# Attention slots 6 to 12 with one visit each: values in 64x32 tiles beside the next slot's scores

## The chip, the cores and the metric

The kernel runs on one core of one Trainium2 chip. The metric is the device time of one execution in microseconds; lower is better. A core has a matrix engine (TensorE, PE in the profile; its weight loads are PEld), a vector engine (VectorE, DVE), a scalar engine (ScalarE, ACT), a general engine (GpSimd, POOL) and a queue for DMAs (SyncE, SP). The matrix engine works out of on-chip memory (SBUF) into eight accumulator banks (PSUM).

## What is computed

```python
q, k, v: (8, 12, 448, 64)            # batch, heads, sequence, head width
q_n, k_n = rmsnorm(q, g_q), rmsnorm(k, g_k)
scores = 1 / sqrt(64) * q_n @ k_n.T
attn = exp(scores - max) / (sum(exp) + 1e-09)
x = (attn @ v) as (3584, 768)         # token, head * width
h = x @ w_in                          # (768, 2048)
out = (h - tanh(h)) @ w_out           # (2048, 768), float32
```

The weights come as float64; the kernel makes float32 of their two words.

## The kernel before

**Slots.** The attention is cut into 48 slots, one for each batch and pair of heads, six to a batch (`NP` = 6). A slot's probabilities stand with keys on the partitions: three full chunks of 128 keys (c = 0, 1, 2) and 64 last keys (c = `KF` = 3), whose 448 queries are folded into two halves of 224. Scores (`scores`, matmuls L567) are made by tiles of 64x32: 64 rows are one head's width, 32 columns a quarter of the keys, so eight tiles work at once. The exponential (L573, ScalarE) takes them from PSUM to the tiles `p`, `p_full` and `p_last`. The values (`last_values`, L621; `values`, L671; `half_values`, L633) multiply them by v. The sums of the exponentials are either made on TensorE by a matmul with ones (`totals`, L694) and inverted on VectorE (L699), or, from slot 13 on, on VectorE and ScalarE (`fold` and what follows it). `divide` multiplies the values by the inverted sums and writes x.

**Two ways for the values.** `values` uses tiles of 128x32 (all 128 keys of a chunk at once) with 224 columns moving, one bank for each half of the queries. `visit`, which slots from `FOLDED` = 13 on use, has tiles of 64x32 as the scores have: each half of a chunk's keys goes to a bank of its own (`half_values`), 448 columns moving, and the matmuls stand in waves between those of the next slot's scores. The two banks then hold two partial sums, so `divide` copies the first to SBUF on ScalarE (L755), adds the second on VectorE (L756) and then multiplies (L760).

**The order of the work** is written out by hand: `first_slot` for slots up to 5, `early_slot` for 6 to 11, `slot` from 12 on. Between its steps each calls `run(ns)`, which issues so much of the MLP, a generator of matmuls priced at its TensorE time. A slot has about four gaps of MLP (`gap_ns`). In slots 6 to 8 the MLP is the first product of batch 0 (`hidden`, matmuls L839, in seven block products p in the order 1, 5, 6, 2, 3, 7, 4 on three banks, whose results VectorE takes at L908 to L922 and ScalarE at L886 and L906); in slots 9 to 11 it is `project_first` (L1256), 96 matmuls of 448 columns, 16 to a bank, copied by ScalarE (L1262) and turned by VectorE (L948). From slot 12 it is batch 1.

**What else runs there.** Weight pieces are loaded (L287, L291, on SP, into three raw buffers), rounded by ScalarE (L71, L72), then VectorE (L78, L79, L82), then GpSimd (L90), after which the raw buffer may be loaded anew. VectorE makes sums of weight blocks (L354, L378 to L381). For the slots to come, q and k are loaded (L101 to L125) four slots ahead and v two, squared by ScalarE (L130, L131), reduced by VectorE (`norm`, L140, L141), brought to the power -1/2 by GpSimd (L142), scaled (`norm_q`, L452 on ScalarE for slots 9 to 14) and turned (`turn`, L465 and L469). From slot 10 on the sums of the full chunks are made on VectorE first (`add`, L598 and L604; `add_last`, L611), and `totals` has only those to multiply. In the last three slots of batch 1, `divide` also sets off four sums of x on GpSimd (L791).

**Banks.** Five banks (`sc`) turn round for scores, totals, turns and values, three (`mm`) for the MLP. Before slot 12 the last two of the five become `av_banks`, for values alone, and three remain to turn round.

The steps of `early_slot(s)` before the change: `totals(s)`, scores of s+1 for chunks 0 and 1, load of v, a gap, turn of s+2, squares of s+3, loads of q and k, a gap, scores of s+1 for the last keys, values of s, `divide(s)`, scores of chunk 2, then half a gap ahead of each of `add`, `add_last`, `norm` and `norm_q`.

Of the kernel before, what the change touches and what calls it, by code (L numbers as in the profile page):

```python
# [13 lines left out]
ALU = mybir.AluOpType  # L14
# [130 lines left out]
def bounded_path(tc, ctx, q, k, v, moe_w_in, moe_w_out, out, g_col, ident, ones, half_ones, neg_half, early):  # L145
# [74 lines left out]
    def load(s, names):  # L220
        b, hp = steps[s]
        for name in names:
            src = {"q": q, "k": k, "v": v}[name]
            if s == 0 and name != "v":
                t = early[name]
            else:
                if name == "v":
                    t = nat.tile([P, 2, NCH, D], F32, name="v_nat", bufs=3)
                elif name == "q":
                    rows = loaded["rows", s] = qk_rows()  # L230
                    t = rows[:CP, : 2 * NCH * D].rearrange("p (h c d) -> p h c d", h=2, c=NCH)
                else:
                    rows = loaded.pop(("rows", s))
                    t = rows[:, 2 * NCH * D :].rearrange("p (c h d) -> p c h d", c=NCH, h=2)
                fetch(nc, name, t, src[b, 2 * hp : 2 * hp + 2], in_order(s))
            loaded[name, s] = t
# [200 lines left out]
    def squares(s):  # L437
        squares_of(nc, early["sq"], early["n"], loaded["q", s], loaded["k", s])
# [42 lines left out]
    def by_blocks(s):  # L481
        return has(s) and s >= TURNED
# [67 lines left out]
    def sc_bank():  # L550
        return bank_of("sc")
# [61 lines left out]
    def last_values(s, av):  # L613

        v_nat, p = loaded["v", s], probs[s, KF]
        for n in range(2):
            keys, at = slice(n * KR, (n + 1) * KR), n * HS if s >= FOLDED else 0
            for m in range(2):
                for h in range(2):
                    r = (2 * m + h) * BL  # L620
                    nc.tensor.matmul(  # L621
                        av[n][r : r + BL, at : at + HS], lhsT=v_nat[keys, h, KF, m * BL : (m + 1) * BL],
                        rhs=p[keys, h, 0], start=(s < FOLDED), stop=False, skip_group_check=(s >= FOLDED),
                    )

    def half_values(s, c, av, first):
# [52 lines left out]
    def totals(s, dn):  # L679

        parts = [t[:, h, n * HS : (n + 1) * HS] for t in sums.get(s, ()) for n in range(2) for h in range(2)]
        parts = [(parts, [ones[:, :BL]] * 2)] if parts else []
        if not sums.pop(s):
            for p in full(s):
                parts.append(
                    ([p[:, h, n * HS : (n + 1) * HS] for n in range(2) for h in range(2)], [ones[:, :BL]] * 2)
                )
            last = probs[s, KF]
            parts.append(([last[:, h, 0] for _ in range(2) for h in range(2)], [half_ones[:, n] for n in range(2)]))
        for i, (moving, by) in enumerate(parts):  # L690
            for n in range(2):
                for h in range(2):
                    r = (2 * n + h) * BL
                    nc.tensor.matmul(  # L694
                        dn[r : r + BL, :HS], lhsT=by[n], rhs=moving[2 * n + h],
                        start=(i == 0), stop=(i == len(parts) - 1),
                    )
        rs = whole[s] = sp.tile([P, HS], F32, name="rs")
        nc.vector.reciprocal(rs, dn[:, :HS])  # L699


    FOLDED = 2 * NP + 1

    def fold(s):

# [41 lines left out]
    def divide(s, av):  # L747
        b, hp = steps[s]
        rs = whole.pop(s)
        if b > PAIRED and b % 2 and hp == 1:  # L750
            x = xT[b, hp] = late["blocks"].tile([P, S], F32, name="xT_more", bufs=1)
        else:
            x = xT[b, hp] = xp.tile([P, S], F32, name="xT")
        if s >= FOLDED:
            nc.scalar.copy(out=x, in_=av[0][:, :S])  # L755
            nc.vector.tensor_tensor(out=x, in0=x, in1=av[1][:, :S], op=ALU.add)  # L756
        for m in range(2):
            rows = slice(m * D, (m + 1) * D)
            if s >= FOLDED:
                nc.vector.tensor_tensor(out=x[rows], in0=x[rows], in1=rs, op=ALU.mult)  # L760
                continue
            for n in range(2):
                nc.vector.tensor_tensor(
                    out=x[rows, n * HS : (n + 1) * HS], in0=av[n][rows, :HS], in1=rs[n * D : (n + 1) * D],
                    op=ALU.mult,
                )
        for c in range(NCH):
            del probs[s, c]
        if b < PAIRED and hp >= HC:
            c = hp - HC  # L770
            x_sums(b, (c,), range(4), nc.vector if b == 0 and c == HC - 1 else nc.gpsimd)
# [526 lines left out]
    def run(ns):  # L1298

        spent[1] += ns  # L1300
        while spent[0] + 1.0 < spent[1]:
            took = next(stream, None)
            if took is None:
                return
            spent[0] += took
# [15 lines left out]
    def has(s):  # L1321
        return 0 <= s < NS
# [40 lines left out]

    def early_slot(s):
        gap = gap_ns(s)
        totals(s, sc_bank())
        if has(s + 1):
            scores(s + 1, 0)
            scores(s + 1, 1)
        if has(s + 2):  # L1370
            load(s + 2, "v")
        run(gap)
        if has(s + 2):
            turn(s + 2, sc_bank(), sc_bank())
        if has(s + 3):
            squares(s + 3)
        if has(s + 4) and not by_blocks(s + 4):
            load(s + 4, "qk")
        run(gap)
        if has(s + 1):  # L1380
            scores(s + 1, KF)
        av = [sc_bank() for _ in range(2)]
        last_values(s, av)
        divide(s, values(s, av))
        if has(s + 1):
            scores(s + 1, 2)
        for work, n in ((add, 1), (add_last, 1), (norm, 3), (norm_q, 3)):
            run(gap / 2)
            if has(s + n):
                work(s + n)  # L1390

    def slot(s):

        gap = gap_ns(s)
        av = av_banks
        if has(s + 1):
            scores(s + 1, KF)
        if s < FOLDED:
            last_values(s, av)
            totals(s, sc_bank())  # L1400
            divide(s, values(s, av))
            for c in range(KF):
                scores(s + 1, c)
        else:
            visit(s, av)
        if has(s + 2):
            load(s + 2, "v")
        rows, ahead, following = has(s + 2), has(s + 3), has(s + 1)
        folded = following and s + 1 >= FOLDED
        first = s + 3 == TURNED  # L1410
        scaled = rows and not first
        if scaled:
            power_blocks(s + 2)
        work = (
            (
                (following, lambda: add(s + 1, False)), (first, lambda: turn(s + 2, sc_bank(), sc_bank())),
                (ahead and not first, lambda: load_blocks(s + 3)),
            ),
            (
                (following, lambda: add_third(s + 1)), (first, lambda: load_blocks(s + 3)),  # L1420
                (True, lambda: x_sums_later(s, 0)),
            ),
            ((following, lambda: add_last(s + 1)),),
            ((folded, lambda: fold(s + 1)),),
            ((folded, lambda: fold_rest(s + 1)), (True, lambda: x_sums_later(s, 1))),
            ((scaled, lambda: scale_blocks(s + 2)),),
            ((folded, lambda: gather(s + 1, 0)), (ahead, lambda: square_blocks(s + 3))),
            ((scaled, lambda: turn_blocks(s + 2, 0)), (folded, lambda: gather(s + 1, 1))),
            ((scaled, lambda: turn_blocks(s + 2, 1)), (ahead, lambda: norm_blocks(s + 3))),
            ((folded, lambda: spread_sums(s + 1)), (True, lambda: x_sums_later(s, 2))),  # L1430
            ((scaled, lambda: weigh_keys(s + 2)), (ahead, lambda: meet_blocks(s + 3))),
            ((folded, lambda: widen_sums(s + 1)),),
            ((folded, lambda: turn_sums(s + 1)),),
            (),
        )
        for point in work:
            run(4 * gap / (len(work) + 1))
            for wanted, fn in point:
                if wanted:
                    fn()  # L1440
        run(4 * gap / (len(work) + 1))
# [4 lines left out]
    done[0] = 1  # L1446
    for s in range(-3, NP):
        first_slot(s)
    for s in range(NP, 2 * NP):
        early_slot(s)  # L1450
    banks["sc"], av_banks = banks["sc"][:3], banks["sc"][3:]
    for s in range(2 * NP, NS):
        slot(s)
    run(1e9)
# [345 lines left out]
```

## Time and profile before

| | us |
|---|---|
| median of three runs | 1360.98 (1359.57 to 1361.94) |
| the profiled execution | 1361.07 |
| its span in the profile | 1359.3 |
| TensorE busy | 1318.1 (97%) |
| VectorE busy | 956.4 (70%) |
| ScalarE busy | 557.4 (41%) |
| GpSimd busy | 762.9 (56%) |
| start of slots 8, 9, 10, 11 and 12 on TensorE | 145.1, 176.0, 208.8, 240.6, 272.3 |

The page has the busy time of each engine, the span in 40 slices of 34 us with the busy share in tenths, the chain of work that ended last, and groups of instructions by line. A matmul of float32 appears as two. "TensorE <- VectorE L910" reads: idle until that instruction ended. Lines of the timeline give start, length, engine, source line, operation, what is written and read, and in brackets the idle time ahead of it with its releaser. TensorE's clock was at its full rate through slots 6 to 12.

### The profile page before, as it was taken

The page shows a single profiled execution, that of the slowest core. Times are in us where ns is not written, and L with a number is a line of the kernel's source. Part 1 is how long each engine was busy: PE and PEld are TensorE (multiplying, and loading weights), DVE is VectorE, ACT ScalarE, POOL GpSimd, SP SyncE. Part 2 cuts the span into 40 slices and gives each one's busy share as a digit, 9 for nine tenths or more (in the row PEclk, how much of TensorE's full clock was granted, in tenths as well). Part 3 has the DMA queues.
Part 4 walks back from the last instruction along what each step waited for, and adds up shares of the span by engine and source line. Part 5 has one row for each costly group of instructions (what it writes and reads, how often), then busy time and mean ns, then how long its engine had stood idle before and what let it go on. Part 6 is the DMA issues. An engine that isn't in the chain of part 4 may idle for free.

```text
span 1359.3 us, 29138 instructions
## 1 busy us (share of the span) xinstructions
PE 1318.1 (97%) x11336; PEld 1028.3 (76%) x11336; DVE 956.4 (70%) x1393; ACT 557.4 (41%) x1326; POOL 762.9 (56%) x559
## 2 busy tenths in 40 slices
PE   7988999999999999999999999999999999999996
PEld 3466854478998888687788787778787888699984
DVE  5999989756865677587887576768786668433553
ACT  7855654244343454445322446354512254211100
POOL 4756665347846246726698235843699153712760
PEclk9999999999999999999999999999999999999998
DMA  7878889879999766466555867475645865365544
GB/s 172 189 201 251 265 257 240 251 247 284 324 290 278 184 159 177 111 184 158 162 143 139 201 165 179 108 179 163 167 140 137 166 193 163 94 171 181 165 140 79
DMA packets 371687, 253.53 MB, mean 187 GB/s; under 512 B 282196, under 2 KB 310228, under 8 KB 371540
## 3 DMA queue, kind: packets, MB, share of 16 engines
q1 hardware_dynamic: 371536, 251.57, 67.2%
q8 instruction: 92, 1.51, 0.5%
q14 instruction: 55, 0.45, 0.1%
q10 hardware_dynamic: 4, 0.00, 0.0%
HBM read 205.23 MB, written 46.27 MB: 185 GB/s over the span
## 4 chain that ended last, share of the span: by engine, by line
PE 82%; DVE 10%; DMA 2%; SPq 2%; issue 1%; ACT 1%; POOL 1%; DVEq 0%; ACTq 0%; POOLq 0%
PE mm L839 35%; PE mm L1092 23%; PE sc L567 8%; PE sc L633 6%; PE mm L1256 5%; DVE xT L760 2%; DMA w_raw<-in_moe_w_in_dram 1%; PE sc L671 1%; DVE rows L611 1%; PE sc L621 1%; DVE rows L604 1%; DVE rows L598 1%; DVE sum_T L708 1%; SPq L125 1%; SPq L287 1%
## 5 line engine op out<-in xcount | busy, mean ns | idle before, releaser
L839 PE MATMUL mm<-xT,w_f 128*128 128x224 f32 x1296 | 264.0, 353 | 1.1 <-DVE s L910 0.7
L839 PEld LDWEIGHTS mm<-xT,w_f 128*128 128x128 f32 x1296 | 244.4, 190 | 7.2 <-issue 5.5
L567 PE MATMUL sc<-qT,kT 64*32 64x448 f32 (+1 forms) x3072 | 213.3, 498 | 2.7 <-ACT p_last L573 1.5
L839 PE MATMUL mm<-tt,w_f 128*128 128x224 f32 x1044 | 213.7, 356 | 0.6
L839 PEld LDWEIGHTS mm<-tt,w_f 128*128 128x128 f32 x1044 | 194.9, 190 | 18.9 <-issue 15.6
L521 POOL TENSOR_TENSOR rr_mine<-rr_mine,neg_half 128x28 f32<-128x28 f32 x33 | 160.6, 4866 | 2.8
L756 DVE TENSOR_TENSOR xT<-xT,sc 128x448 f32<-128x448 f32 x32 | 19.9, 621 | 177.6 <-PE sc L567 119.4
L1092 PE MATMUL mm<-u,w_f 128*128 128x224 f32 x672 | 136.5, 354 | 1.2 <-DVE sum_all L731 1.0
L887 POOL TENSOR_TENSOR gT<-s,th 128x448 f32<-128x448 f32 x44 | 55.8, 1270 | 144.9 <-ACT th L886 141.7
L1092 PE MATMUL mm<-gT,w_f 128*128 128x224 f32 (+1 forms) x480 | 133.0, 429 | 3.1 <-DVE acc L1099 3.0
L1092 PEld LDWEIGHTS mm<-u,w_f 128*128 128x128 f32 x672 | 126.1, 190 | 8.2 <-POOL u L1049 3.8
L567 PEld LDWEIGHTS sc<-qT,kT 64*32 64x32 f32 x3072 | 70.8, 106 | 70.1 <-issue 51.7
L1092 PEld LDWEIGHTS mm<-gT,w_f 128*128 128x128 f32 x480 | 90.2, 190 | 40.6 <-issue 34.2
L633 PE MATMUL sc<-p,v_nat 64*32 64x448 f32 x1120 | 110.5, 536 | 0.0
L1092 PE MATMUL mm<-g,w_f 128*128 128x224 f32 (+1 forms) x360 | 99.5, 428 | 1.1 <-DVE acc L1099 1.1
L723 ACT COPY sum_g<-sum 32x14 f32<-32x14 f32 x280 | 56.3, 201 | 105.8 <-DVE sum L715 100.1
L573 ACT ACTIVATE p<-sc 128x448 f32<-128x448 f32 x132 | 71.7, 543 | 50.3 <-PE sc L567 42.4
L887 POOL TENSOR_TENSOR g<-s,th 128x448 f32<-128x448 f32 x24 | 30.3, 1265 | 108.5 <-ACT th L886 93.6
L1092 PEld LDWEIGHTS mm<-g,w_f 128*128 128x128 f32 x360 | 67.9, 190 | 28.1 <-issue 26.2
L1256 PE MATMUL mm<-gT,w_out 128*128 128x448 f32 x192 | 74.3, 542 | 0.0
L142 POOL TENSOR_TENSOR rr<-rr,neg_half 112x8 f32<-112x8 f32 (+1 forms) x30 | 49.1, 1667 | 32.7 <-DVE rr L141 32.3
L1049 POOL TENSOR_TENSOR u<-gT 128x448 f32<-128x448 f32 x48 | 59.1, 1252 | 11.1 <-PE mm L1092 11.1
(196 smaller groups left out, 2424.0 us busy)
## 6 DMA issues: line engine op xcount, KB each, us to landing
w_f<-w_in SPq DMA_DIRECT2D x196, 384.0 KB, 3.4
w_f<-w_inner SPq DMA_DIRECT2D x63, 512.0 KB, 3.5
w_f<-w_out SPq DMA_DIRECT2D x42, 512.0 KB, 3.8
w_raw<-in_moe_w_out_dram SPq DMA_DIRECT2D x16, 768.0 KB, 5.5
w_in<-w_out SPq DMA_DIRECT2D x21, 384.0 KB, 5.2
qk_nat<-in_q_dram SPq DMA_DIRECT2D x132, 56.0 KB, 2.9
qk_nat<-in_k_dram SPq DMA_DIRECT2D x132, 56.0 KB, 2.3
g<-w_out SPq DMA_DIRECT2D x14, 512.0 KB, 4.7
```

The lines of the kernel that those rows point to most:

```text
L142: nc.gpsimd.tensor_tensor(out=r, in0=r, in1=neg_half[:rows], op=ALU.pow)
L521: nc.gpsimd.tensor_tensor(out=mine, in0=mine, in1=neg_half[:, :1].to_broadcast([P, 2 * NJ]), op=ALU.pow)
L567: nc.tensor.matmul(tiles[h][i * BL : (i + 1) * BL, :n], lhsT=kT[r, c * P + at : c * P + at + BL], rhs=qT[r, first : first + n], start=True ...
L573: nc.scalar.activation(p[:, h, c if c < 2 else 0, :], tiles[h][:, :n], AF.Exp, scale=1.0 if rr is None else rr[:, 0, 2 * c + h : 2 * c + h ...
L633: nc.tensor.matmul(av[g][i * BL : (i + 1) * BL, :S], lhsT=v_nat[keys, h, c, m * BL : (m + 1) * BL], rhs=p[keys, h], start=first, stop=True ...
L723: nc.scalar.copy(out=acc[h * BL : (h + 1) * BL, g], in_=part[g * BL : (g + 1) * BL, h * NJ : (h + 1) * NJ])
L760: nc.vector.tensor_tensor(out=x[rows], in0=x[rows], in1=rs, op=ALU.mult)
L839: nc.tensor.matmul(bank[:, f * HS : (f + 1) * HS], lhsT=w[:, c * width + f, :], rhs=moving[p](c), start=(first and f == 0 and c == 0), sto ...
L887: eng.tensor_tensor(out=g[:, rows, cols], in0=h, in1=th, op=ALU.subtract)
L1049: nc.gpsimd.tensor_tensor(out=u[:, half], in0=a[:, half], in1=z[:, half], op=ALU.subtract)
L1092: nc.tensor.matmul(bank[:, :n], lhsT=w(i), rhs=mv, start=(first and i == 0), stop=(i == len(moving) - 1), skip_group_check=not first,)
L1256: nc.tensor.matmul(bank[:, :S], lhsT=w_out_row(f, n // HC)[:, n % HC * P : (n % HC + 1) * P], rhs=g[:, f, :], start=(f == 0), stop=(f == C ...
```

## The change

Slots 6 to 12 (from `HALVED` = 6) have their values made by `visit`, and the constant takes `FOLDED`'s place where the two bank layouts differ; their sums stay on TensorE. `early_slot` begins with the scores of the last keys and the visit, loads v behind it, and calls `totals(s + 1)` two and a half gaps into slot s, so that `divide` of the next slot finds the inverted sums; slot 6 makes its own at its start. `norm` moves from the third gap's end to the second's, `norm_q` to the third's. The split of the five banks moves from ahead of slot 12 to ahead of slot 6.

```diff
@@ last_values
-            keys, at = slice(n * KR, (n + 1) * KR), n * HS if s >= FOLDED else 0
+            keys, at = slice(n * KR, (n + 1) * KR), n * HS if s >= HALVED else 0
...
-                        rhs=p[keys, h, 0], start=(s < FOLDED), stop=False, skip_group_check=(s >= FOLDED),
+                        rhs=p[keys, h, 0], start=(s < HALVED), stop=False, skip_group_check=(s >= HALVED),
@@
-    FOLDED = 2 * NP + 1
+    HALVED, FOLDED = NP, 2 * NP + 1
@@ divide
-        if s >= FOLDED:
+        if s >= HALVED:
             nc.scalar.copy(out=x, in_=av[0][:, :S])
             nc.vector.tensor_tensor(out=x, in0=x, in1=av[1][:, :S], op=ALU.add)
...
             for n in range(2):
+                part_of = x[rows, n * HS : (n + 1) * HS]
                 nc.vector.tensor_tensor(
-                    out=x[rows, n * HS : (n + 1) * HS], in0=av[n][rows, :HS], in1=rs[n * D : (n + 1) * D],
-                    op=ALU.mult,
+                    out=part_of, in0=part_of if s >= HALVED else av[n][rows, :HS],
+                    in1=rs[n * D : (n + 1) * D], op=ALU.mult,
                 )
@@ early_slot
-        totals(s, sc_bank())
-        if has(s + 1):
-            scores(s + 1, 0)
-            scores(s + 1, 1)
-        if has(s + 2):
-            load(s + 2, "v")
+        if s == NP:
+            totals(s, mm_bank())
+        scores(s + 1, KF)
+        visit(s, av_banks)
+        load(s + 2, "v")
         run(gap)
-        if has(s + 2):
-            turn(s + 2, sc_bank(), sc_bank())
-        if has(s + 3):
-            squares(s + 3)
-        if has(s + 4) and not by_blocks(s + 4):
+        turn(s + 2, sc_bank(), sc_bank())
+        squares(s + 3)
+        if not by_blocks(s + 4):
             load(s + 4, "qk")
+        run(gap / 2)
+        add(s + 1)
+        run(gap / 2)
+        add_last(s + 1)
+        norm(s + 3)
+        run(gap / 2)
+        totals(s + 1, sc_bank())
+        run(gap / 2)
+        norm_q(s + 3)
         run(gap)
+
+    def slot(s):
+
+        gap = gap_ns(s)
         if has(s + 1):
             scores(s + 1, KF)
-        av = [sc_bank() for _ in range(2)]
-        last_values(s, av)
-        divide(s, values(s, av))
-        if has(s + 1):
-            scores(s + 1, 2)
-        for work, n in ((add, 1), (add_last, 1), (norm, 3), (norm_q, 3)):
-            run(gap / 2)
-            if has(s + n):
-                work(s + n)
-
-    def slot(s):
-
-        gap = gap_ns(s)
-        av = av_banks
-        if has(s + 1):
-            scores(s + 1, KF)
-        if s < FOLDED:
-            last_values(s, av)
-            totals(s, sc_bank())
-            divide(s, values(s, av))
-            for c in range(KF):
-                scores(s + 1, c)
-        else:
-            visit(s, av)
+        visit(s, av_banks)
...
+    banks["sc"], av_banks = banks["sc"][:3], banks["sc"][3:]
     for s in range(NP, 2 * NP):
         early_slot(s)
-    banks["sc"], av_banks = banks["sc"][:3], banks["sc"][3:]
     for s in range(2 * NP, NS):
         slot(s)
```

## The prediction

> **What bounds the kernel now.** First the busy shares and slices of the page. TensorE (PE) is busy for 97% of the span, but VectorE (DVE) stands at 9 and 8 tenths from slice 1 to slice 6, some 34 to 240 us, just where the slots of the change lie.
>
> ```profile
> PE 1318.1 (97%) x11336; PEld 1028.3 (76%) x11336; DVE 956.4 (70%) x1393; ACT 557.4 (41%) x1326; POOL 762.9 (56%) x559
> DVE  5999989756865677587887576768786668433553
> ```
>
> Then the busy times by stretch: slot 6 and most of slot 7; the rest of 7 and slot 8; slots 9, 10, 11. Columns are PE, weight load, DVE, ACT, POOL.
>
> ```profile
> 74.00:124.00 50.00, 41.26 (x404) 32.76 (x397) 48.95 (x66) 26.09 (x47) 28.74 (x15) 1.00 0.81 235
> 124.00:179.00 55.00, 54.96 (x531) 45.24 (x529) 52.45 (x71) 34.02 (x60) 34.31 (x20) 1.00 0.83 255
> 179.00:209.00 30.00, 30.00 (x182) 15.15 (x176) 23.71 (x25) 18.50 (x34) 17.26 (x12) 1.00 0.83 241
> 209.00:240.00 31.00, 31.00 (x207) 15.40 (x200) 28.69 (x39) 14.87 (x30) 17.49 (x11) 1.00 0.93 242
> 240.00:272.00 32.00, 32.00 (x210) 15.56 (x208) 24.17 (x43) 9.21 (x22) 10.31 (x8) 1.00 0.88 251
> ```
>
> Up to 124 us VectorE is the bound (48.95 of 50) and TensorE waits 8.7 us in all; from 124 to 179 both are full; from 179 TensorE alone. The reader keeps two things: TensorE time is worth its full price only from slot 9 on, and up to slot 8 each VectorE microsecond is on the path.
>
> Third, the chain of waits for slot 11, and for slot 16, which has a visit already (start, length, what).
>
> ```profile
> 240.57 0.52 PE sc L694 x8
> 241.08 1.66 PE sc L567 x32
> 242.75 6.21 PE mm L1256 x16
> ...
> 255.81 0.54 PE sc L567 x16
> 256.35 0.38 PE sc L621 x16
> 256.73 2.41 PE sc L671 x48
> 259.13 0.91 PE sc L567 x16
> 260.05 12.22 PE mm L1256 x32
> ```
>
> ```profile
> 385.47 0.54 PE sc L567 x16
> ...
> 390.15 0.75 PE sc L567 x16
> 390.90 21.76 PE mm L839 x114
> ```
>
> Slot 11 spends 1.66+0.54+0.38+2.41+0.91 = 5.90 on scores and values, a visit 390.90-385.47 = 5.43.
>
> Last, ScalarE (ACT) where slot 9 begins; TensorE wrote the scores that L573 takes here from 177.6 on.
>
> ```profile
> 180.15 0.93 ACT L71 ACTIVATE w_out<-w_raw 128x768 f32<-128x768 f32 x1 [2.57 <-DMA w_raw<-in_moe_w_out_dram]
> ...
> 182.25 2.00 ACT L452 ACTIVATE n<-qk_nat,rr 112x64 f32<-112x64 f32 x8
> 184.15 2.17 ACT L573 ACTIVATE p<-sc,rr 128x448 f32<-128x448 f32 x4
> ```
>
> The exponentials (exps) come 6.5 us late, behind the rounding of a weight piece that waits for its load. With five score banks TensorE had gone on to the MLP and lost nothing.
>
> **Two rules.** The Trainium skill, "TensorEngine Tiling (Array Packing)", Tiling Modes, says that changing the tile shape drains TensorE, and gives no price. The trace agrees: eight waves of 64x32 scores take 1.50 inside a visit and 1.66 after 128x32 totals; one chunk 0.75 against 0.91. So one switch costs 0.16, and I go by the trace. "TensorE: Matmul & The Clock Gate", Architectural detail, says that ScalarE and VectorE are strict FIFO; the rows above show it, exps ready since 178 standing behind a rounding. The forecast's waits rest on that.
>
> **What the change does, priced.** All in us.
>
> (a) TensorE. An early slot has now seven shape switches around totals, scores and values; afterwards the visit has two and the totals two. Chain: 5.90 becomes 5.43; totals keep 0.5 (1.65 with sums on TensorE) but stand alone, and the return to the MLP costs about 0.2 (6.21 against 6.03), which another interruption gives back. Slot 10, 31.77 now (208.80 to 240.57), becomes 5.43 + turn 0.83 + totals 0.54 + 64 matmuls of 128x448 at 0.373 (23.9) + returns 0.5 = 31.2: -0.6; slot 11 -0.5. Slot 9 now has totals of 1.65, which move into slot 8, and takes 0.54 instead: 32.84 to 31.2, -1.65. Slot 12 runs from 272.27 to 280.54, with three exps waited for; afterwards 5.43, its totals being in slot 11: -2.8. These slots are bound by TensorE, so all counts: **-5.55**.
>
> (b) VectorE and ScalarE. L763 is four times 0.39 = 1.6. It becomes a ScalarE copy (L755, 0.527), an add (L756, 0.62) and the same four products; their in0 now lies in SBUF, for which L791 at 128x224 shows 0.39 too. So +0.62 of VectorE a slot: in slots 6 to 8, 1.9. The reciprocal (L699, 1.55) and the key norms (2 x 0.67 + 2 x 0.17 = 1.7) also move ahead of MLP work. In slot 8, matmul group p=7 starts at 171.2 and waits for L910, done at 170.35: slack 0.9. In front of L910 stand 1.9 + 1.7 = 3.5 more, so p=7 is 2.6 late. TensorE alone would reach slot 9 at +0.3 (one more totals, 1.8, less three savings of 0.5). Slot 9 starts between +0.3 and +3.4 (all of 1.9+1.55); I take **+2.3**. Two waits of the turn for L699 (L465 idle 1.28 and 2.61, at 85 and 124), whose bank it shares, go, as other banks come round; next late is L910, done at 124.0 for a p=7 at 125.24, so they bring nothing while VectorE is the bound. No gain below +0.3: TensorE's own work stands there.
>
> (c) Visit of slot 9. Scores have three banks, so the second wave pair of chunk 0 needs the exp of the last keys, 2.04 after the visit starts (0.54+0.75+0.75). The visit starts at 175.96+2.3 = 178.3; ScalarE must first do the rounding of 180.15, whose load waits for POOL (L90) behind VectorE, so 1 to 2 later than now, and a tanh: first exp done at 183 to 184.5. Wait 2.7 to 4.1, less what load and queue may win: bounds 0 and 4; **+2.5**.
>
> (d) Totals of slot 10 need L611 of that slot. VectorE does after the visit's end (t): copy and division to t+2.8, rounding of pieces 23 and 24 (2.1 to 3.6 each: L78, L79, L82, longer when POOL works), L598 and L604 (2.2 to 3.7), L948 behind the bank that ends at t+13, L611 1.3 to 2.8: done at t+15.8 to 18. TensorE is there at t+15.9 (20 matmul steps of 0.747, turn 0.83). Bounds 0 and 2; **+0.4**.
>
> (e) Visit of slot 10. Now VectorE rounds piece 25 at 197.0, right behind the division of slot 9; ScalarE ends piece 28, which takes the same raw buffer, at 209.95, 10.1 after piece 25 left VectorE (POOL 203.03, load issued 203.06, landed 208.2). Afterwards L948, L611 and the norms stand in front of piece 25, so it ends 19.6 after t and piece 28 at t+29.7. The visit starts at t+26.3 and needs its exp at t+28.3; it comes at t+30.6. Bounds 0 and 4; **+2.2**.
>
> (f) Totals of slot 11. Piece 28's VectorE part stands behind the division (t+2.8 to 4.9), POOL's part behind four sums of slot 10 that the division now sets off there (L791, 4.5 together), load 31 (5.5), ScalarE, VectorE again (2.7), L948, L611: t+18.5 to 20.6, against t+15.9. Bounds 0 and 5; **+3.0**. In slot 11 the MLP sums L378 to L381 (1.95 per four steps) leave L611 at t+15.8: nothing.
>
> (g) SP, POOL. The v loads move behind the visit, 5 later, for a visit two slots on: nothing, 20 us cover it. If that cover went, a visit would wait for its landing (5.4). The qk loads stay. POOL's powers (2 x 1.6) move a gap earlier and give the query norms more time. Slots 13 on are as before and bound by TensorE, so the shift stays to the end.
>
> Sum: -5.55 + 2.3 + 2.5 + 0.4 + 2.2 + 3.0 = +4.9. The profiled execution took 1361.07 (span 1359.3 and 1.8 around it), 0.1 over the median of the three runs, 1360.98. Forecast **1366.0**, from 1363.8 to 1369 by itself.
>
> **Rivals.**
> 1. *The switches decide.* If the exps of slots 9 and 10 come within 2.04 of their visit's start and L611 within 15.9 of the visit's end, (c) to (f) are nothing: -5.55 + 2.3 = -3.2, or -5.2 if VectorE's lag isn't felt either: 1355.8 to 1358. For it: VectorE and ScalarE idle in slots 9 and 11 (23.7 of 30, 24.2 of 32), and every visit since slot 13 costs just 5.43. Against: piece after piece waits for its load (SP waited 37.7 for POOL in ten places from 140 to 215).
> 2. *Half the waits.* The lag of slot 8 and the first visit count, (e) and (f) don't, since a wait in slot 9 gives loads time: -5.55+2.3+2.5+0.4 = -0.35: 1360.7.
> 3. *Three banks are too few.* ScalarE is late in visits 7, 8, 11 and 12 too, each by some 1.5: +4.9+6 = +10.9: 1372. Against: norms come earlier than now and slots 11 and 12 have no rounding.
>
> **How the numbers follow.** Forecast 0.5, rival 1 0.2, rival 2 0.2, rival 3 0.1. A measurement of this kernel tells about 0.2%, 2.7 us, from no change: rival 1 is faster, rival 2 within, forecast and rival 3 slower. Cases of both signs have weight: the forecast's own range is 1363.8 to 1369; the range that holds 8 in 10 goes from 1357.5, inside rival 1, to 1370.
>
> **What would show it.** Slot 12's first MLP matmul 5.4 after its visit begins, and one piece of scores and values of 5.43 in slot 11: (a) right. TensorE's start of slot 9 against 175.96, less or more than +2.3: (b). In the visits of slots 9 and 10 a wait of L567 for ACT: (c), (e); in the totals of slots 10 and 11 a wait of L694 for DVE L611: (d), (f). If these waits are under 1 us together, the forecast is wrong and rival 1 holds; it is also wrong if slots 6 to 8 end early.

## The result

The changed kernel took **1375.47 us** (median of 6 runs, 1374.69 to 1376.85) against 1362.05 for the kernel before (6 runs): ratio 1.0101, 95% interval 1.0091 to 1.0111, or +13.4. The side was right; the forecast of 1366.0 was 9.5 too low, and its upper end 1370 was passed. The profiled execution has a span of 1373.5 against 1359.3, +14.2. (In the changed kernel lines from 757 on are numbered one higher: L908 is L909.)

The page first: TensorE's busy time rose by 4.1, VectorE's by 10.8 with seven instructions more; the rest of the 14.2 is TensorE waiting.

```profile
PE 1322.2 (96%) x11336; PEld 1029.0 (75%) x11336; DVE 967.2 (70%) x1400; ACT 563.9 (41%) x1333; POOL 760.6 (55%) x559
DVE  5999988767756676768787668587787577534453
```

The busy times by stretch of the changed kernel (PE, weight load, DVE, ACT, POOL, then TensorE's granted clock, the DMA share and GB/s): roughly slot 7, slot 8 and slot 10.

```profile
115.00:153.00 38.00, 31.79 (x281) 26.45 (x281) 37.34 (x43) 22.44 (x40) 22.18 (x14) 0.96 0.90 255
153.00:188.00 35.00, 34.55 (x332) 26.18 (x331) 31.79 (x41) 22.10 (x39) 19.75 (x12) 0.95 0.80 250
220.00:256.00 36.00, 30.00 (x168) 14.43 (x152) 30.57 (x39) 16.04 (x31) 18.26 (x12) 0.91 0.81 211
```

In slot 7 VectorE is full (37.34 of 38). Slot 10, which was TensorE's alone before (31.00 of 31), is no longer anyone's: TensorE stands still for 6 of 36, at a clock of 0.91. TensorE's waits of the changed kernel from 70 to 310 us (in all, times, longest) say for what:

```profile
PE sc L694 <- DVE rows L611: 5.0, 1, 5.0
PE mm L840 <- DVE s L909: 5.0, 1, 5.0
PE mm L694 <- DVE rs L699: 4.3, 1, 4.3
PE mm L840 <- DVE s L911: 3.3, 3, 1.7
PE sc L567 <- ACT p_last L573: 2.1, 2, 1.1
PE mm L840 <- DVE s L919: 1.9, 1, 1.9
PE mm L840 <- DVE s L923: 0.6, 1, 0.6
```

Three waits of 4.3 to 5.0 stand out: slot 6's totals for the reciprocal of slot 5 (L699), slot 7's MLP for L909, slot 11's totals for L611. The chain of the changed kernel for the last of them and for slot 12:

```profile
245.11 1.60 DVE rows L611
246.72 0.14 issue
246.85 1.52 PE sc L694 x8
248.38 11.06 PE mm L1257 x24
...
280.93 0.54 PE sc L694 x8
281.47 9.22 PE mm L1257 x24
290.69 0.54 PE sc L567 x16
...
296.12 1.71 PE mm L840 x8
```

The same 8 totals and 24 MLP matmuls take 1.52 and 11.06 behind the wait for L611, 0.54 and 9.22 a slot later: the wait of 5.0 is followed by 2.8 at a lower clock. The granted clock behind it (last but two in each row):

```profile
246.00:248.00 2.00, 1.15 (x8) 0.40 (x8) 1.94 (x3) 0.00 (x0) 0.23 (x1) 0.50 1.03 286
248.00:251.00 3.00, 3.00 (x7) 1.47 (x5) 2.93 (x7) 0.97 (x4) 2.64 (x2) 0.50 0.76 144
```

Slot 12's MLP begins 5.43 after its visit, as forecast.

Slot by slot on TensorE (visit or totals to the next; slot 12 up to its MLP):

| | before | after | difference | forecast |
|---|---|---|---|---|
| start of slot 6 | 75.06 | 77.38 | +2.3 | |
| slot 6 | 35.30 | 37.92 | +2.6 | |
| slot 7 | 34.71 | 38.27 | +3.6 | |
| slot 8 | 30.82 | 31.53 | +0.7 | |
| start of slot 9 | 175.89 | 185.10 | **+9.2** | +2.3 (b) |
| slot 9 | 32.84 | 33.26 | +0.4 | -1.65+2.5+0.4 |
| slot 10 | 31.77 | 41.01 | **+9.2** | -0.6+2.2+3.0 |
| slot 11 | 31.70 | 31.25 | -0.5 | -0.5 |
| slot 12 to its MLP | 8.27 | 5.43 | -2.8 | -2.8 |

Up to there the changed kernel is 15.6 behind where +4.9 was forecast, and at VectorE's last instruction 16.0 (it ends at 1364.28 instead of 1348.25). The span grows by only 14.2 because what follows that instruction took 9.2 instead of 11.1 in this execution.

### The profile page after: what moved, and what is told of

Read it like the earlier page. It is cut to its first block, busy times and chain, and to the rows that moved or that the text cites. A ratio compares the mean times of both kernels' runs of the same rounds, so it can differ in the third digit from the quotient of the medians.

```text
span 1373.5 us, 29147 instructions
## 1 busy us (share of the span) xinstructions
PE 1322.2 (96%) x11336; PEld 1029.0 (75%) x11336; DVE 967.2 (70%) x1400; ACT 563.9 (41%) x1333; POOL 760.6 (55%) x559
## 4 chain that ended last, share of the span: by engine, by line
PE 77%; DVE 13%; DMA 3%; issue 2%; POOL 1%; ACT 1%; SPq 1%; DVEq 0%; POOLq 0%
PE mm L840 33%; PE mm L1093 23%; PE sc L567 9%; PE sc L633 6%; PE mm L1257 3%; DVE xT L760 2%; DVE rows L611 1%; PE sc L621 1%; DMA w_raw<-in_moe_w_out_dram 1%; DVE w_out L79 1%; DVE rows L604 1%; PE mm L671 1%; DVE rows L598 1%; DVE w_out L82 1%; DVE w_out L354 1%
## 5 line engine op out<-in xcount | busy, mean ns | idle before, releaser
L840 PEld LDWEIGHTS mm<-xT,w_f 128*128 128x128 f32 x1296 | 245.5, 191 | 11.5 <-DVE s L909 5.6
L567 PE MATMUL sc<-qT,kT 64*32 64x448 f32 (+1 forms) x3072 | 223.8, 500 | 4.2 <-ACT p_last L573 3.6
L756 DVE TENSOR_TENSOR xT<-xT,sc 128x448 f32<-128x448 f32 x39 | 24.2, 621 | 196.2 <-PE sc L567 134.6
L633 PE MATMUL sc<-p,v_nat 64*32 64x448 f32 x1344 | 135.5, 537 | 0.0
L567 PEld LDWEIGHTS sc<-qT,kT 64*32 64x32 f32 x3072 | 76.7, 107 | 70.3 <-issue 51.0
L633 PEld LDWEIGHTS sc<-p,v_nat 64*32 64x32 f32 x1344 | 49.2, 107 | 37.6 <-issue 37.6
```

The costliest lines, as they stand in the source:

```text
L567: nc.tensor.matmul(tiles[h][i * BL : (i + 1) * BL, :n], lhsT=kT[r, c * P + at : c * P + at + BL], rhs=qT[r, first : first + n], start=True ...
L633: nc.tensor.matmul(av[g][i * BL : (i + 1) * BL, :S], lhsT=v_nat[keys, h, c, m * BL : (m + 1) * BL], rhs=p[keys, h], start=first, stop=True ...
L840: nc.tensor.matmul(bank[:, f * HS : (f + 1) * HS], lhsT=w[:, c * width + f, :], rhs=moving[p](c), start=(first and f == 0 and c == 0), sto ...
```

## The experiments

Two theories stood at the start. **Lag:** VectorE is the bound up to slot 9 and late in slots 9 and 10; every wait comes from its queue. **Clock and banks:** the waits are made by the three score banks and by the clock behind them. The kernels, each against the runs of before on its own chip:

| kernel | us | ratio to before, interval |
|---|---|---|
| slot12_only | 1360.09 | 0.9994, 0.9987 to 1.0001 |
| from_slot9 | 1369.92 | 1.0064, 1.0047 to 1.0081 |
| totals_at_start | 1401.06 | 1.0291, 1.0274 to 1.0309 |
| from_slot9_start | 1379.38 | 1.0143, 1.0114 to 1.0171 |
| bank_sc | 1381.44 | 1.0138, 1.0115 to 1.0162 |
| no_add | 1373.48 | 1.0092, 1.0065 to 1.0119 |
| clock_fill | 1373.56 | 1.0084, 1.0065 to 1.0104 |
| add_last_early | 1368.86 | 1.0052, 1.0033 to 1.0071 |
| norm_late | 1380.97 | 1.0144, 1.0126 to 1.0161 |
| both_orders | 1374.07 | 1.0093, 1.0077 to 1.0109 |
| normq_behind | 1372.53 | 1.0092, 1.0075 to 1.0109 |
| normq_behind_early | 1367.33 | 1.0038, 1.0025 to 1.0051 |
| from_slot9_early | 1365.44 | 1.0030, 1.0023 to 1.0037 |
| from_slot11 | 1361.63 | 1.0000, 0.9991 to 1.0010 |
| from_slot11_behind | 1360.21 | 0.9993, 0.9984 to 1.0001 |
| from_slot10_behind | 1361.20 | 0.9999, 0.9991 to 1.0007 |
| from_slot11_free | 1360.21 | 0.9990, 0.9982 to 0.9998 |
| from_slot10_free | **1357.67** | **0.9975, 0.9969 to 0.9982** |

### Which slots lose

from_slot9 leaves slots 6 to 8 as before (`plain_slot` is the old `early_slot`); slot 9 makes its own totals at its start.

```diff
-    HALVED, FOLDED = NP, 2 * NP + 1
+    HALVED, FOLDED = NP + 3, 2 * NP + 1
-        if s == NP:
-            totals(s, mm_bank())
+        if s == HALVED:
+            totals(s, sc_bank())
...
+    for s in range(NP, HALVED):
+        plain_slot(s)
```

> The kernel after, but slots 6 to 8 as they were; the visits, and the totals ahead, begin with slot 9, which makes its own totals at its start. Theory: slot 9 starts where it did before the change (+0 in place of +9.2), slot 9 costs +2, slot 10 +9 through the wait for L611 and the clock, slots 11 and 12 give back 3.3: 1362 + 8 = 1370. Rival (all of the loss comes from slots 6 to 8, where VectorE is full): 1359 to 1360.

1369.92, as the theory said: slots 9 to 12 alone lose some 8.6, against 13.4 in all. Slot 9's visit is 10.0 long (2.9 of it a wait for L699), slot 10's 7.51, the totals of slot 11 wait 4.95, and 1.52 and 10.67 follow at the lower clock. Visit 10 and the wait for L611 are those of the changed kernel, though slots 6 to 8 are not late here: the second loss doesn't come from the first.

Lengths of visits in these sections run to the end of the last matmul, 0.07 beyond the start of the next one; a visit without waits is 5.50 long by that count and 5.43 by the other.

slot12_only is the kernel before with the visit in slot 12 alone and its totals at its start.

> The kernel before, with one visit in slot 12 alone (its totals at the slot's start, 128x32 values in slots 6 to 11). Theory (waits in VectorE's queue, each followed by a slow clock): none of these places is touched, so slot 12 shrinks from 8.27 to 0.68 + 5.43 = 6.1 us and the whole comes to 1362.05 - 2.2 = 1359.9. Rival (three banks are too few for a visit): exponentials of slot 12 are late, its visit takes 7 us or more, 1361 to 1363.

1360.09, near the theory's time, but the visit took 7.1, with a wait of 1.4 for L699. A gain within what can be told from none.

### Totals ahead, or in their own slot

totals_at_start moves the totals of every slot back to its own start, in a score bank; from_slot9_start does so with visits from slot 9 on; bank_sc only for slot 6.

```diff
-        if s == NP:
-            totals(s, mm_bank())
+        totals(s, sc_bank())
         scores(s + 1, KF)
...
-        totals(s + 1, sc_bank())
-        run(gap / 2)
```

> The kernel after, but the totals of slots 6 to 12 stand at the start of their own slot, ahead of the visit, in a score bank. Theory: the wait for L611 in slot 10 (5.1) and the slow clock behind it (3.0) go, so does the wait of slot 6's totals for a reciprocal (2.5); the reciprocal no longer stands ahead of L909 in slot 7. 1375.5 - 8 - 2.5 - 1 to 2 = 1363 to 1364. Rival (three banks): visits cost what they did, 1373 to 1375.

> Both: visits from slot 9 on, totals at each slot's start. Theory: neither VectorE's full stage nor the wait for L611 is touched; slots 9, 10, 11 give 0.5 each if the exponentials are in time, or lose 1.5 in slots 9 and 10 if they are as late as in the kernel after; slot 12 gives 2.2. 1358 to 1361. Rival (three banks): at least 2 lost in each visit of slots 9 to 11, 1364 or more.

> The kernel after, with the totals of slot 6 in a score bank instead of an MLP bank. Theory: the wait of 4.27 for the reciprocal of slot 5, whose bank it shares, goes, and VectorE no longer waits 1.7 for the first visit; VectorE is the bound behind it, so 1.7 to 4 are gained: 1371.5 to 1374. Rival (VectorE's lag of slots 7 and 8 takes back whatever the start gives): no change, 1375.5.

All three theories missed by far, in one way; from_slot9_start fell to its rival, three banks. TensorE's waits of totals_at_start from 70 to 320:

```profile
PE sc L567 <- DVE rs L699: 32.5, 6, 7.9
```

With three score banks the visit comes round to the totals' bank within itself, and that is free only when VectorE has inverted it. VectorE's queue is that late: visits took 7.5 to 16.4 instead of 5.5; in bank_sc the first one waited 7.96 and took 15.8; most of the remaining 2.3 is the clock, 0.50 from 86 to 89. So the part of the change that makes the totals three eighths of a slot ahead is what makes three banks bearable at all; the MLP bank that slot 6 borrows costs a wait of 4.3, a score bank one of 8.

### VectorE's work and the clock

no_add leaves the addition of the second half of the keys out of slots 6 to 12.

```diff
             nc.scalar.copy(out=x, in_=av[0][:, :S])
-            nc.vector.tensor_tensor(out=x, in0=x, in1=av[1][:, :S], op=ALU.add)
+            if s >= FOLDED:
+                nc.vector.tensor_tensor(out=x, in0=x, in1=av[1][:, :S], op=ALU.add)
```

> The kernel after, without the sum of the two value banks in slots 6 to 12 (L756 left out there, so half the keys are lost in these slots). Theory: VectorE, the bound from slot 6 to 8, has 3 times 0.62 less to do, and the wait of slot 7 for L909 shortens by 1.2: 1.5 to 3 less, 1372.5 to 1374. Rival (the order in VectorE's queue counts, not the amount): within 0.7 of 1375.5.

1373.48. The interval reaches that of the changed kernel, so the time alone settles nothing; in the trace the first totals to slot 9 take 106.0 instead of 107.7, against the 1.9 that VectorE lost there. That this is the price (b) gave the add isn't shown, for the clock differs too: visit 8 took 5.50 here, 6.90 in the changed kernel. Either way most of the 9.2 is left unexplained.

clock_fill issues 14 matmuls of 128x448 ahead of the totals of slot 11, where TensorE waits anyway.

```diff
+        dn = sc_bank()
+        if s == 2 * NP - 2:
+            for f in range(7):
+                nc.tensor.matmul(dn[:, :S], lhsT=ident, rhs=late["g"][:, f, :], start=True, stop=True)
-        totals(s + 1, sc_bank())
+        totals(s + 1, dn)
```

> The kernel after, with 14 matmuls of 128x448 (identity by g, 5.2 us, into the bank that the totals then overwrite) ahead of the totals of slot 11, where TensorE waits 4.97 for L611. Theory (the wait is followed by a slow clock): totals and MLP behind it take 0.6 and 9.2 instead of 1.52 and 11.13: 1375.5 - 2.9 = 1372.6. Rival (no price beside the wait itself): 1375.5 to 1375.8.

1373.56, again too near to tell by the time. The trace tells; chain of clock_fill:

```profile
240.79 5.26 PE sc L1386 x14
246.05 0.83 PE sc L694 x8
246.88 9.22 PE mm L1257 x24
```

And its granted clock in the two stretches shown above for the changed kernel:

```profile
246.00:248.00 2.00, 2.00 (x12) 0.94 (x12) 1.90 (x6) 0.00 (x0) 0.75 (x1) 1.00 1.04 261
248.00:251.00 3.00, 3.00 (x9) 1.52 (x8) 3.00 (x4) 2.02 (x8) 3.00 (x3) 1.00 0.38 56
```

Kept busy, TensorE does the totals in 0.83 and the MLP in 9.22. The stand itself made the 2.5 behind it. The Trainium skill, "TensorE: Matmul & The Clock Gate", Part 1, puts half rate behind at least one idle window of some 3.4 us, and says that the windows run freely. The traces agree on the rate, 0.50, and for long waits: in those of all the kernels from 66 to 326 us, each of the 25 waits of 4.0 to 8.0 was followed by a mean clock of 0.50 to 0.70 over the next 1.5 us. For shorter waits the figure of 3.4 doesn't decide. Behind 3.4 (slot 6's totals in norm_late and normq_behind) the clock stayed at 1.00; behind 2.6 (the same totals in no_add and add_last_early) and 2.8 (normq_behind_early, where they took 3.11 instead of 1.72) it fell to between 0.50 and 0.63; and behind one and the same wait of 2.5 in slot 6's MLP it was 1.00 in the kernel before and 0.50 in from_slot9_early. What a wait adds is so 0 to 3, and below 4 us its length alone doesn't say which.

### The wait for L611

add_last_early puts L611 right behind L604, half a gap earlier.

```diff
         run(gap / 2)
         add(s + 1)
+        add_last(s + 1)
         run(gap / 2)
-        add_last(s + 1)
         norm(s + 3)
```

> The kernel after, with L611 right behind L604, half a gap earlier, ahead of the rounding of the last weight pieces in VectorE's queue. Theory: the wait of 4.97 in slot 10 and the slow clock behind it (2.9) go: 1367.6. Rival (VectorE has the same work to do and some other wait comes in its place): 1373 or more.

1368.86: the totals of slot 11 no longer wait (0.59), the MLP behind takes 9.76, and 6.6 of the 13.4 are gone (7.4 of slot 10 in the trace): the 5.0 of the wait and nearly all that followed it. No other wait takes its place there.

### Where the norms stand

norm_late moves the norms back by a gap, to three gaps into the slot, and norm_q by half a gap, to three and a half (before the change, by its code, they stood three and a half and four gaps in); both_orders has add_last_early's order too.

```diff
         add_last(s + 1)
-        norm(s + 3)
         run(gap / 2)
         totals(s + 1, sc_bank())
         run(gap / 2)
+        norm(s + 3)
+        run(gap / 2)
         norm_q(s + 3)
-        run(gap)
+        run(gap / 2)
```

> The kernel after, with norm and norm_q back at three and three and a half gaps, where they were before the change. Theory (order in VectorE's queue): in slot 7, L909 no longer stands behind the norms (2.7 us there), its wait falls from 4.95 to about 2.3[...]: 1375.5 - 5 = 1370.5, if the query norms on ScalarE aren't late for the next visit. Rival (ScalarE): exponentials of visits 7 to 10 come behind norm_q, 1375 to 1380.

> As norm_late, and L611 right behind L604 as well. Theory: the two gains are in different slots and add: norm_late's time less 6.6. Rival: as for norm_late, about 1369 to 1373.

norm_late's theory missed and its rival, ScalarE, held: 1380.97, slower still. Slots 6 and 7 did lose their waits for L919 and L923 and most of that for L909 (1.0 instead of 5.0), so the norms do stand in its way; but four visits now wait for ScalarE. TensorE's waits of norm_late from 70 to 310:

```profile
PE sc L567 <- ACT p_last L573: 12.8, 4, 4.6
PE sc L694 <- DVE rows L611: 5.0, 1, 5.0
...
PE mm L840 <- DVE s L909: 1.0, 1, 1.0
```

The visits of slots 7 to 10 are 11.5, 12.4, 12.1 and 8.2 long. both_orders is 6.9 below norm_late: the gain of an early L611 adds.

normq_behind tests why: the norms stand as in norm_late, and norm_q is issued behind the next visit, a gap ahead of its turn. normq_behind_early adds the early L611.

```diff
         visit(s, av_banks)
+        if s > HALVED:
+            norm_q(s + 2)
         load(s + 2, "v")
...
-        norm_q(s + 3)
```

> The changed kernel with the key and query norms half a gap behind the totals, as in norm_late, and the scaling of the query norms (norm_q, L452) no longer at the slot's third gap but behind the next visit, a gap ahead of the turn that needs it. If the visits of norm_late were long because L452 stands ahead of the exponentials and waits for GpSimd's power, visits 7 to 9 go from 11.5 to 12.4 back to 5.5 to 7.5, and since VectorE has the norms no longer ahead of L909, slots 6 to 8 are 4 to 5 shorter than in the changed kernel: 1369.5 to 1371.5, the wait for L611 in the totals of slot 11 still there. If ScalarE is late for another reason (pieces of weights), visits stay over 9: 1376 to 1381.

> The same with add_last right behind add. The gains add if they are separate: 6.6 less than normq_behind, 1363 to 1365. If the wait for L611 was made only by the lag of slots 6 to 8, nothing is added: 1369.5 to 1371.5.

1372.53 and 1367.33, 1.0 and 2.3 above what was expected, but well below norm_late and both_orders. L452 was one half of it, the load of a weight piece the other: visit 7's first exp comes at 115.95 instead of 118.26, still behind a rounding (L71) that waited 2.69 for its load, and the visit took 10.2, the end of it at a clock of 0.62. Visit 8 is 5.50 again and visit 10 5.74. And slot 9 now starts at 178.35, **+2.8** against the kernel before. It is the size that (b) forecast, but not by its route: slot 6 starts 3.3 late, and slots 6 to 8 together take 100.0, against 100.8 before and 107.7 in the changed kernel. Of the 6.7 so gained up to slot 9, 5.6 are lost again in the visit of slot 9, which takes 13.1.

from_slot9_early shows that visit without any lag: slots 6 to 8 as before, slot 8 makes the totals of slot 9, visits from slot 9 on, L611 early.

```diff
+    HALVED, FOLDED = NP + 3, 2 * NP + 1
...
             if has(s + n):
                 work(s + n)
+            if s + 1 == HALVED and work == norm:
+                totals(s + 1, sc_bank())
```

> Slots 6 to 8 as before the change, but slot 8 makes the totals of slot 9 three and a half gaps in; visits from slot 9 on, with L611 right behind L604. Theory: nothing is left of VectorE's waits; slots 9 and 10 give 0.5 each and lose up to 2 each to a late exponential, slot 11 gives 0.5, slot 12 2.8: 1357.5 to 1361.5. Rival (visits in slots 9 to 11 cost on their own): 1364 or more.

A miss for the theory; the rival's range holds: 1365.44. The visit of slot 9 begins at 177.89. ScalarE's timeline in from_slot9_early (start, length, engine, line, what, idle time ahead):

```profile
180.24 0.91 ACT L71 ACTIVATE w_out<-w_raw 128x768 f32<-128x768 f32 x1 [2.52 <-DMA w_raw<-in_moe_w_out_dram]
...
182.30 2.00 ACT L452 ACTIVATE n<-qk_nat,rr 112x64 f32<-112x64 f32 x8
184.20 0.76 ACT L573 ACTIVATE p_last<-sc,rr 128x224 f32<-128x224 f32 x2
```

That is the queue of the kernel before, to a tenth of a microsecond (its L71 at 180.15, L452 at 182.25, first exp at 184.15): the piece's load sets it, not TensorE. There five banks let TensorE go on; here three don't. The stretches of this visit:

```profile
177.89:180.70 2.81, 2.81 (x51) 1.01 (x50) 2.74 (x5) 0.46 (x1) 1.73 (x2) 1.00 1.07 386
180.70:184.60 3.90, 0.01 (x1) 0.00 (x0) 1.46 (x2) 3.90 (x13) 2.89 (x3) 0.98 0.86 301
184.60:187.60 3.00, 2.91 (x32) 1.56 (x40) 0.00 (x0) 1.52 (x4) 0.64 (x2) 0.50 0.91 287
```

TensorE works for 2.8 and stands for 4.0, and what remains of the visit, 2.6 in a bare one, takes 5.1. The visit is 11.9 long, 6.4 too much: 4.0 is the wait, some 1.5 the clock (3.0 at half the rate, an estimate from the last row), and some 0.9 smaller stands behind the later exps. In normq_behind 5.4 is the wait and 2.2 the rest. In the changed kernel, with a wait of 1.1, the clock stays at 1.00, and the visit is 2.0 too long. In all three the last rounding ahead of the first exp waited for its load, 2.52, 2.44 and 0.90 long. Side by side, the visit of slot 9:

| | visit starts | first exp | exp after start | visit's length | MLP goes on |
|---|---|---|---|---|---|
| after | 185.10 | 188.54 | 3.4 | 7.5 | 192.6 |
| from_slot9_early | 177.89 | 184.20 | 6.3 | 11.9 | 189.8 |
| normq_behind | 178.35 | 186.08 | 7.7 | 13.1 | 191.4 |

The earlier TensorE gets there, the longer it waits. Moving slot 9's start by 6.7 to 7.2 moves the end of its visit by 1.1 to 2.8.

### Few slots, and what stood in their way

from_slot11 has visits in slots 11 and 12 only; from_slot11_behind adds norm_q behind the visit, the early L611 and the totals of slot 11 half a gap earlier; from_slot10_behind the same from slot 10 on.

> Slots 6 to 10 as before the change, slot 10 makes the totals of slot 11 three and a half gaps in; visits in slots 11 and 12. Theory: slot 11 gives 0.5, slot 12 2.8, as they do in the kernel after, and no wait is added: 1361.7 - 3.3 = 1358.4. Rival (some wait takes the gain): 1360.5 to 1362.

> Slots 6 to 10 as before, visits in 11 and 12 only; add_last right behind add, the totals of slot 11 at the third half-gap point, and norm_q behind the visit. In from_slot11 the visit of slot 11 lost 1.25 to L699, which stood behind the norms on VectorE, and the last keys of slot 10's visit 1.3 to a rounding on ScalarE. The first goes, the second stays: 1.2 less than from_slot11, 1359.5 to 1360.5. If L699 is as late as before: 1361 to 1362.

> The same with visits from slot 10 on. One more slot saves 0.6 on TensorE, and its visit waits for a piece of weights on ScalarE by up to 2: 1359 to 1361.5. If both lose nothing, 1358.

from_slot11 missed (1361.63): 1.25 went in slot 11's visit (6.75; L699 stood behind four key-norm instructions and a weight sum on VectorE) and 1.4 in the last keys of slot 10 (exps behind a piece's rounding), about what the switches gave. from_slot11_behind has both visits at 5.50 (1360.21), within what can't be told from no change. from_slot10_behind has all three at 5.50 and yet gains nothing (1361.20): slot 10's totals wait 2.0 for L611, and slot 12's turn, now close behind norm_q, takes 2.0 instead of 1.0.

from_slot10_free and from_slot11_free take these away: norm_q of slot 14 is back in slot 11 (by the code right behind the totals, two and a half gaps in, with its norm at two; not shown in the cut below), and in from_slot10_free slot 10's totals, which slot 9 makes, come half a gap later.

```diff
     def plain_slot(s):
...
         add(s + 1)
         add_last(s + 1)
-        run(gap / 2)
+        run(gap)
         totals(s + 1, sc_bank())
-        run(gap / 2)
         norm(s + 3)
```

> from_slot11_behind, with the norms of slot 14 at the third gap and its norm_q at three gaps and a half of slot 11, so that the turn in slot 12 no longer waits for L452 (in from_slot11_behind the turn took 2.0 instead of 0.98). If the switches' gain of slots 11 and 12 counts in full: 1 less, 1359.0 to 1359.6. If slot 12's visit now waits for L452: 1360.2 to 1361.

> from_slot10_behind with the same for slot 14, and the totals of slot 10 half a gap later, so that their wait for L611 (2.0) is under 1. If these waits held the gain: 2 to 3 less, 1358 to 1359.2. If they only give way to a wait of slot 10's visit for L699 or ScalarE: 1360 to 1361.5.

from_slot10_free took **1357.67**, ratio 0.9975, interval 0.9969 to 0.9982: 3.4 better than before by the ratio, a little beyond its expectation, and the only version clearly better than both kernels. Its chain:

```profile
205.82 0.52 PE sc L694 x8
206.34 3.20 PE mm L1257 x8
209.54 0.54 PE sc L567 x16
...
214.22 0.82 PE sc L567 x16
```

No wait ahead of the totals, a visit of 5.5, and from the start of slot 9 to the MLP of slot 12 101.94 instead of 104.58. from_slot11_free (1360.21, 0.9990) fell in its upper expectation, though slot 12's visit waited for nothing (5.50); the same stretch takes 102.90. No run has the new orders of from_slot10_free without its visits, so how much of the gain is theirs isn't shown.

## Why the prediction was right in side and wrong in size

The sum came to 15.6 instead of 4.9 for two terms: (b) was 6.9 too small and (f) 4.8. What both lacked is the low clock behind a stand of TensorE, 2.8 in (f) and up to 4.7 in (b); (b) also had the wrong waits, (f) a wait of 5.0 for 3.0. Of the two theories of the start each has its part: the waits come from late queues, and the banks and the clock decide what a late queue costs.

(a) **right.** Slot 11 -0.5, slot 12 -2.8, slot 9 -1.6 without its waits, visits of 5.43 wherever nothing waits. from_slot10_free turns the gain into time: (a) without slot 9 is -3.9; slot 9 takes 0.7 more there, for the totals of slot 10: -3.2, against 2.6 gained in the trace (slot 10's last MLP took 9.7 instead of 9.2) and 3.4 in the time.

(b) **too small: +9.2, not +2.3.** The step took VectorE's added work, 3.5 in front of L910 against a slack of 0.9, and looked only at slot 8. Three things were missed. First, slot 6's totals, which had no term in the sum, borrow an MLP bank that holds slot 5's totals, and wait 4.3 for their reciprocal: slot 6 is 2.3 late before it begins. Second, the norms stand ahead of L909 already in slot 7, together with the reciprocal and two weight sums that took 2.6 each. VectorE's queue in the changed kernel:

```profile
138.27 0.68 DVE L140 TENSOR_REDUCE rr<-n 112x8 f32<-112x512 f32 x1
...
143.00 5.29 DVE L354 TENSOR_TENSOR w_out<-w_out,w_out 128x768 f32<-128x768 f32 x2
148.21 1.54 DVE L699 RECIPROCAL rs<-sc 128x224 f32<-128x224 f32 x1
149.68 0.56 DVE L909 TENSOR_TENSOR s<-mm,s 128x448 f32<-128x448 f32 x1
```

TensorE waits for that L909 from 145.3 to 150.3. The instructions are those of the step, but it put their turn a slot too late. Third, the clock behind these two waits: scores and totals of slot 6 take 1.65 more, MLP of slot 7 1.65, visit of slot 8 1.4. The share of slot 6 counts in full: clock_fill is the same kernel up to slot 10, but in its trace the first wait was 3.1 and the clock stayed at 1.00, and slot 6 took 36.26 instead of 37.92 while slots 7 and 8 took the same (38.18 and 31.55). How much of the 3.05 of slots 7 and 8 would have been hidden under a full VectorE isn't settled. normq_behind, with the norms out of L909's way and the clock at 1.00 behind both waits, loses nothing in slots 6 to 8 but the late start.

(c) **right in place; that +2.0 came for +2.5 is luck.** The step counted on a start of slot 9 at 178.3, and it came at 185.1 because (b) failed. Where it does start there, in normq_behind, the visit takes 7.6 too much. The two terms can't be priced separately: an earlier slot 9 waits longer for an exp that a load sets. The step's upper bound of 4 is the wait of from_slot9_early, 4.0; the further 2.4 behind it, the clock and the later exps, had no term. The grace was 2.8 rather than 2.04.

(d) +0.4 forecast, none measured. (e) right: +2.2 forecast, 2.0 measured (visit 7.46), with the first exp behind the rounding of a piece that waited 3.58 for its load.

(f) **right in place, mis-sized: 5.0 for 3.0, and 2.8 more behind it.** The wait is the upper bound of the step; the lower clock (totals 1.52 for 0.54, MLP 11.06 for 9.22) was no term of the sum at all. add_last_early gets 6.6 of the 7.8 back.

(g) right: no visit waits for v.

Rival 1 (the switches decide) didn't hold for seven slots; in three, from slot 10 on and with the waits taken away, its mechanism does. That from_slot10_free ends at 1357.67, inside the 1355.8 to 1358 that rival 1 gave for seven slots, is chance. Rival 2 (half the waits) fell with (e) and (f), which came in full. Rival 3's mechanism, three banks too few, is what the totals_at_start kernels show; its place was wrong, since in the changed kernel visits 7, 11 and 12 didn't wait for ScalarE.

What stays open: the share of the clock in slots 7 and 8, what decides the clock behind waits of under 4 us, and what the new orders of from_slot10_free would do without the visits.

## What to carry to other kernels

A change that saves time on one engine by giving it fewer banks also takes its run-ahead away: price it in the stage by how late the other engines' queues are there, and not by the work it adds. In this case every wait of TensorE of 4 us or more was followed by a low clock, which cost 1.5 to 3 where it was compared; a forecast of such a wait needs a term for both. Where a saving vanishes, move it to the slots that no other engine holds: the visits in three slots of seven, with the order around them mended, gained 0.25% where in all seven they lost 1.0%.

## What had not been expected of the hardware

A stand of TensorE of 4.0 to 5.0 us cost 1.5 to 3 more in the matmuls behind it (8 totals 1.52 for 0.54, 24 matmuls 11.06 for 9.22, at a granted clock of 0.50); filling it with 14 further matmuls took 2.5 of that away. Below 4 us it was chance as far as these traces tell: one and the same wait of 2.5, in a stage that both kernels share, was followed by a clock of 1.00 in the kernel before and of 0.50 in from_slot9_early, where the stretch of MLP around it took 9.65 instead of 8.21. Two profiles of the same stage can so differ by 1.4 for the clock alone.
